# A round-ordered mixer kernel: weight steps ahead of kv's split in every attention round, the gated MLP's PSUM banks a on the other side, and one left operand made in the fourth gated batch

## The chip, the cores and the metric

The kernel runs on one core of one Trainium2 chip. The metric is the device time of one execution in microseconds (us): the median of the runs that are shown. TensorE multiplies matrices, VectorE and ScalarE do elementwise work and read TensorE's results from PSUM, GpSimd does elementwise work in SBUF, and SyncE's queue (SP) issues nearly all transfers. Each engine works through its own instructions in the order in which they were written into its queue, so an instruction that waits holds up all that stands behind it on that engine.

## The reference, cut to what matters

Three layers follow each other, for 8 batches of 576 tokens and 512 channels (8 heads of 64):

```
phi(x) = [exp(p - max|p|), exp(-(p - max|p|))], p = x @ w_phi     # 64 -> 128 features
kv = phi(k)^T v;  z = sum phi(k);  x = (phi(q) kv) / (phi(q) z + 1e-6)
h = relu(x @ w_in); u, v = halves of h; v_n = normalized v
x = (u * (w_spatial @ v_n + b_spatial)) @ w_out
u = x + (U V) mixed over tokens;  out = u + relu(u @ w_ch1) @ w_ch2
```

The weights w_in, w_out, w_ch1, w_ch2 and U, V arrive as 64-bit floats and are turned into pairs of 32-bit halves (a high part in the fp32r format, and the rest as a low part), so that a product becomes three products of halves.

## The kernel before, in words

**Attention** goes through 32 pairs of heads in 35 overlapping rounds, `p` from -1 to 33; "round 9" means p = 9. A round projects k and q of the next pair, builds the features of this pair (`key_features`, `high_part`, `low_part`), accumulates kv in the PSUM tile `pkv` (`key_values`), splits it into a high part on ScalarE (L714) and a low part on VectorE (L715) in `split_key_values`, and multiplies the pairs one and two rounds behind (`outputs`: a group of six products into the PSUM tile `pn`, which is then copied out as `nd`, L738 on VectorE and L740 on ScalarE). Everything in a round is pinned: each engine gets it in the order of the code.

Beside it a list of jobs prepares the weights of the gated MLP, one piece of a weight in each round in four steps that `step(work)` calls at four places of the round. Of a piece of w_in the first step is ScalarE's (`words`, L62), the second VectorE's (`rounded`, three instructions on `bits`: L67, L71, L75), the third ScalarE's (`sized`, L80, which overwrites what L75 reads), the fourth VectorE's last one (L87), a cast on ScalarE (L184) and a subtraction on GpSimd (L187). In rounds 9 to 13 the list `rest` is not empty: it holds the loads of the first batch's input x, whose cast (L974, ScalarE) and subtraction into `xs` (L971, GpSimd) come at the end of a round. In those rounds the second step stood behind kv's split, in the others ahead of it.

At the end of attention (`p == n - 1` and later, n = 32) the first value products of the gated MLP are put between the last rounds (`fill`, into the three PSUM banks of a tile `pa`; (t, half) names token tile and half), and `stats` copies a bank to SBUF (`v`, L1007) and computes its mean and variance.

**The gated MLP** then goes through the 8 batches. For each, `gate` computes four blocks f by two halves c of `u` (8 products `pu`), then the same of the spatial product `pz`, multiplies them (`u`, L1090, VectorE) and splits the result into `g` (L184 on ScalarE, L187). The output product `px` follows, then the small mix over tokens (`pr`, `pt`, `py`). PSUM tiles come from two pools of four banks each: `a` (pu, pz, px, pv, pt) and `b` (py, pr); a pool's tiles take its banks in turn, and a tile waits until its bank's earlier tile has been read.

Between the products, `units` plans the weights of the last layer: at a place (batch, place) a step is emitted, where places 0 to 7 lie behind the eight pu, 8 to 15 behind the eight pz, "x" behind the opened output products, "blocks" behind the second output tile, "m1" and "m2" behind the halves of the mix. A *left operand* m (0 to 7) of w_ch1 is loaded from DRAM (`load`), its sums are made on GpSimd (L569), and two parts are split: ScalarE casts into the one staging buffer `w2s` (L426), VectorE makes the low part (L430), and two stores to `w1x` carry it away. The lists in `left(m, loading, where, early, second)` say where: `early` places the cast and the low part of the 768 columns taken over as they are, `second` those of the 1024 columns of sums. As `w2s` exists once, a cast waits until the stores before it have landed.

**The channel layer** (from about 870 us of the span) reads the left operands back and runs two chained products (ph, pc) to the end.

Of the kernel before, what the change touches and what calls it, by code (L numbers as in the profile page):

```python
# [16 lines left out]
PSUM = bass.MemoryType.PSUM  # L17
# [121 lines left out]
class Mixer:  # L139
# [196 lines left out]
    def units(self):  # L336
# [180 lines left out]
        rest = others + [rows(m + i * self.NM) for m in (5, 6, 7) for i in range(2)]  # L517
# [15 lines left out]
        assert not rest  # L533
        for m, *where in (
# [8 lines left out]
        ):  # L543
            left(m, *where)

# [232 lines left out]
    def attention(self, jobs):  # L778

        nc, n = self.nc, self.B * self.NP
        late, rest, work = 2 * self.NP, [], None
        self.pinned = {}
        self.load(0, "k", 2)
        self.load(0, "q", 1)
        self.load(0, "v", 2)
        none = lambda: None

        def step(f, last=False):

            if f and (last or not getattr(f, "late", False)):
                with self.behind():
                    return f()
            return f

        pa = early = begun = None

        def fill(ks):  # L800
            for t, half in ks:
                self.ahead = True
                self.value_products(0, t, early[t], range(2 * half, 2 * half + 2))
                self.ahead = False

        def stats(t):
            self.ahead = True
            self.statistics(0, t, early[t])
            self.ahead = False

        for p in range(-1, n + 3):
            tag = "pn" if p < n else "kv"
            new, this, old, older = (0 <= i < n for i in (p + 1, p, p - 1, p - 2))
            if p + 2 < n:
                self.load(p + 2, "k", 2)
            if p == n - 1:
                pa = self.pp.tile([P, 12, P], F32, tag="pa", name="pv_0", bufs=1)
                early = [
                    pa[:, 4 * t : 4 * t + 4].rearrange("p u f -> p (u f)") for t in range(3)
                ]  # L820
                fill([(0, 0)])
            elif p == n:
                fill([(2, 0)])
            less = (begun or self.project(p + 1, "k")) if new else none
            begun = None
            side = self.key_values(p, 1) if this else iter(())
            taken = self.outputs(p - 2, 2, side, 6) if older else none
            less()
            taken()
            work = step(work)  # L830
            if this:
                self.transposes(p)
            if p == n:
                fill([(2, 1)])
            taken = self.outputs(p - 2, 3, side, 6, tag) if older else none
            for _ in side:
                pass
            if p + 2 < n:
                self.load(p + 2, "v", 2)
            if new:  # L840
                self.key_features(p + 1, 0)
            if not rest:
                work = step(work)
            taken()
            if older:
                self.undivided(p - 2)
            if this:
                self.split_key_values(p)
            if rest:
                work = step(work)  # L850
            if p == n - 1:
                fill([(0, 1), (1, 0)])
            less = self.project(p + 1, "q") if new else none
            if p + 2 < n:
                self.load(p + 2, "q", 1)
            if this:
                self.high_part(p, 0)
                work = step(work)
                self.low_part(p, 0)
            for i in {n + 1: (), n + 2: (n - 2, n - 1)}.get(p, (p - 3,)):  # L860
                if 0 <= i < n:
                    self.finish(i)
            less()
            if p < 0:
                begun = self.project(1, "k")
            side = self.key_values(p + 1, 0) if new else iter(())
            taken = self.outputs(p - 1, 0, side, 3) if old else none
            for _ in range(3):
                next(side, None)
            taken()  # L870
            if p == n - 1:
                fill([(1, 1)])
            taken = self.outputs(p - 1, 1, side, 6, tag) if old else none
            for _ in side:
                pass
            if this:
                self.high_part(p, 1)
            if new:
                self.key_features(p + 1, 1)
            if this:  # L880
                self.low_part(p, 1)
            if getattr(work, "late", False):
                taken()
                taken = none
            work = step(work, True)
            taken()
            if n - 1 <= p <= n + 1:
                stats(p - n + 1)
            if older:
                self.reciprocals(p - 2)  # L890
            rest = [step(f) for f in rest]
            rest = [f for f in rest if f]
            if jobs and not work:
                work = jobs.pop(0)()
            if 0 <= p - late < self.KD:
                rest.append(self.load_x(0, p - late))
        while work or jobs:
            work = work() if work else jobs.pop(0)()


    def alloc_moe(self, left, right):
        tc, nc, NF, tail = self.tc, self.nc, self.NF, self.tail
        self.ps = {
            x: es.enter_context(
                tc.tile_pool(name=f"ps{x}", bufs=1, space=PSUM, reuse_waits="tile")
            )
            for x, es in (("a", self.ctx), ("b", left))
        }
        mp = self.mp = left.enter_context(tc.tile_pool(name="mp", bufs=1, reuse_waits="tile"))
        self.gs = self.gated(0)  # L910
        mq = self.mq = right.enter_context(tc.tile_pool(name="mq", bufs=1, side="right", reuse_waits="tile"))


        self.vn = [mq.tile([P, self.NST, self.DH], F32R, name=f"vn{i}") for i in range(2)]
# [916 lines left out]
```

## Time and profile before

| what | value |
|---|---|
| median of 3 runs | 1578.63 us (1577.75 to 1579.96) |
| the profiled execution: its time, its span | 1578.13 us, 1576.3 us |
| TensorE busy (matmul) | 1548.2 us, 98% |
| VectorE, ScalarE, GpSimd busy | 1129.6, 874.1, 800.5 us |
| granted TensorE clock, mean | 0.998 |
| mean DMA rate | 213 GB/s |

The span is the stretch from the first to the last profiled instruction; 1.8 us of the execution lie outside it. A busy TensorE is a sum of modelled durations, so the time it was idle, and the name of what ended each idle stretch, say more here than its share. A granted clock of 1.00 is the 2.4 GHz level, 0.50 the 1.2 GHz level.

### The profile page before, as it was taken

What the parts mean: (1) busy time and instruction counts of PE and PEld (TensorE: products, weight loads), DVE (VectorE), ACT (ScalarE), POOL (GpSimd) and SP (SyncE); (2) the same over time, 40 slices, a digit from 0 to 9 for tenths busy, and PEclk for the clock granted to TensorE, in tenths of its full rate; (3) what the DMA queues carried; (4) which work ended last, traced back from release to release, by engine and by line L of the source; (5) the groups of instructions that cost most, each with busy time, mean ns of one, the idle gap of its engine ahead of it and who ended that gap; (6) DMA issues with size and microseconds to landing.
All of it is one profiled execution on the core that took longest, in us unless ns stands there. A gap on an engine that the chain in (4) does not pass through costs nothing.

```text
span 1576.3 us, 30493 instructions
## 1 busy us (share of the span) xinstructions
PE 1548.2 (98%) x11592; PEld 1460.7 (93%) x11592; DVE 1129.6 (72%) x1630; ACT 874.1 (55%) x1647; POOL 800.5 (51%) x602
## 2 busy tenths in 40 slices
PE   8999999999999999999999999999999999999999
PEld 7988888998898898998897999999999999999998
DVE  6787766884687786686777677777666666666666
ACT  6788777884454453454444555555545555554443
POOL 3767776776344554454644644345455533345430
PEclk9999999999999999999999999999999999999999
DMA  5676666763253652443648788878999877777785
GB/s 153 189 201 199 187 200 175 206 176 104 92 168 124 217 181 97 144 154 106 196 149 343 254 275 263 275 253 278 306 321 327 295 246 234 239 240 247 246 298 164
DMA packets 167703, 335.82 MB, mean 213 GB/s; under 512 B 25603, under 2 KB 90755, under 8 KB 164997
## 3 DMA queue, kind: packets, MB, share of 16 engines
q1 hardware_dynamic: 167412, 333.81, 66.1%
q8 instruction: 91, 1.49, 0.4%
q14 instruction: 56, 0.45, 0.1%
q10 hardware_dynamic: 144, 0.07, 0.0%
HBM read 251.20 MB, written 73.02 MB: 206 GB/s over the span
## 4 chain that ended last, share of the span: by engine, by line
PE 58%; DVE 4%; DMA 2%; issue 1%; ACT 1%; POOL 0%; SPq 0%; DVEq 0%; ACTq 0%; POOLq 0%
PE pc L935 22%; PE ph_x L935 13%; PE ph_z L935 6%; PE pv L935 3%; PE ph_y L935 3%; PE pz L935 2%; PE pu L935 2%; PE px L935 2%; DVE w2s L430 1%; PE pt L1160 1%; DMA w1x<-w2s 1%; PE py L1164 1%; PE pv L947 0%; DVE xl L187 0%; PE pz L1086 0%
## 5 line engine op out<-in xcount | busy, mean ns | idle before, releaser
L935 PE MATMUL pc<-hc,w 128*128 128x288 f32 x2568 | 406.0, 295 | 0.0
L935 PEld LDWEIGHTS pc<-hc,w 128*128 128x128 f32 x2568 | 363.1, 188 | 0.0
L682 POOL TENSOR_TENSOR qp<-e,qp 128x576 fp32r<-128x576 f32 x128 | 183.6, 1455 | 116.8 <-ACT e L679 102.4
L187 DVE TENSOR_TENSOR hc<-h,hc 128x576 fp32r<-128x576 f32 x192 | 200.0, 1050 | 35.9 <-ACT hc L184 35.2
L935 PE MATMUL ph_x<-us,cw 128*128 128x288 f32 x1344 | 212.2, 294 | 0.1
L729 PE MATMUL pn<-qp,kv 128*65 128x288 f32 x768 | 205.5, 327 | 6.4 <-ACT nd L740 5.7
L935 PEld LDWEIGHTS ph_x<-us,cw 128*128 128x128 f32 x1344 | 189.4, 188 | 0.7 <-ACT u L1415 0.5
L1348 POOL TENSOR_TENSOR t<-u,t 128x576 f32<-128x576 f32 x32 | 57.7, 1802 | 236.4 <-DVE c L1420 213.7
L1415 ACT COPY u<-ph_x 128x288 f32<-128x288 f32 x128 | 51.2, 400 | 201.4 <-PE ph_x L935 200.9
L1348 POOL TENSOR_TENSOR h<-h,h 128x576 f32<-128x576 f32 x60 | 100.3, 1672 | 110.2 <-DVE r L1623 106.7
L701 PE MATMUL pkv<-v,kp 128*128 128x65 f32 x1024 | 152.4, 251 | 0.0
L701 PEld LDWEIGHTS pkv<-v,kp 128*128 128x128 f32 x1024 | 150.8, 190 | 0.0
L184 ACT CAST hc<-h 128x576 fp32r<-128x576 f32 x192 | 128.6, 672 | 5.4 <-PE pc L935 3.8
L1430 ACT ACTIVATE h<-c 128x288 f32<-128x288 f32 x192 | 85.2, 443 | 68.0 <-DVE c L1420 68.0
L935 PE MATMUL pz<-wt,vn 128*128 128x288 f32 x768 | 115.8, 301 | 4.9 <-DVE u L1090 4.9
L935 PEld LDWEIGHTS pz<-wt,vn 128*128 128x128 f32 x768 | 108.2, 192 | 5.9 <-DVE u L1090 5.9
L729 PEld LDWEIGHTS pn<-qp,kv 128*65 128x65 f32 x768 | 98.1, 138 | 11.4 <-ACT nd L740 8.2
L935 PE MATMUL ph_z<-us,cw 128*128 128x288 f32 x672 | 107.1, 295 | 0.1
L935 PEld LDWEIGHTS pu<-xs,wi 128*128 128x128 f32 x768 | 102.8, 188 | 1.2 <-DVE v L1011 0.5
L935 PE MATMUL pu<-xs,wi 128*128 128x288 f32 x768 | 103.5, 295 | 0.3 <-DVE v L1011 0.3
L1623 DVE TENSOR_TENSOR r<-pc,r 128x576 f32<-128x576 f32 x108 | 81.4, 754 | 28.8 <-PE pc L935 28.6
L1019 POOL TENSOR_TENSOR rstd<-rstd,mhalf 128x1 f32<-128x1 f32 (+1 forms) x40 | 30.7, 769 | 138.7 <-DVE rstd L1018 138.7
(180 smaller groups left out, 3266.3 us busy)
## 6 DMA issues: line engine op xcount, KB each, us to landing
w<-w2d SPq DMA_DIRECT2D x214, 512.0 KB, 4.5
u<-ud SPq DMA_DIRECT2D x16, 1152.0 KB, 8.4
raw_c<-in_w_ch SPq DMA_DIRECT2D x32, 512.0 KB, 4.0
v<-in_v SPq DMA_DIRECT2D x32, 325.0 KB, 4.4
k<-in_kT SPq DMA_DIRECT2D x32, 320.0 KB, 3.5
q<-in_qT SPq DMA_DIRECT2D x32, 320.0 KB, 4.1
x<-nd SPq DMA_DIRECT2D x64, 144.0 KB, 3.4
rec<-rd SPq DMA_DIRECT2D x64, 144.0 KB, 3.3
```

The lines of the kernel that those rows point to most:

```text
L184: self.put(nc.scalar.copy(hi, src))
L187: return self.put((nc.gpsimd if elo == "pool" else nc.vector).tensor_tensor(out=lo, in0=src, in1=hi, op=ALU.subtract))
L430: nc.vector.tensor_tensor(out=d[:, 1, k], in0=x, in1=d[:, 0, k], op=ALU.subtract)
L682: self.pin(nc.gpsimd.tensor_tensor(out=lo[:, c], in0=e[:, c], in1=hi[:, c], op=ALU.subtract))
L701: self.pin(nc.tensor.matmul(pkv[:, i, j, :], kp[:, j * NF + t, :], vb[:, u * D1 : (u + 1) * D1], start=False, stop=(j == 1 and t == NF - 1),))
L729: self.pin(nc.tensor.matmul(pn, kv[k][:, i, g // 2, :], qp[q][:, i, g * HS : (g + 1) * HS], start=(m == 0), stop=(m == len(terms) - 1),))
L935: self.put(self.nc.tensor.matmul(out, x, y, start=(start and i == 0), stop=(stop and i == len(terms) - 1), skip_group_check=chained,))
L1019: put(nc.gpsimd.tensor_tensor(out=rstd[:n], in0=rstd[:n], in1=self.mhalf[:n, :1], op=ALU.pow))
L1348: x = self.put(engine.tensor_tensor(out=out, in0=p, in1=q, op=ALU.subtract))
L1415: self.put(nc.scalar.copy(out, src))
L1430: self.put(nc.scalar.activation(self.h[n, t // 2, x][:, t % 2], src, AF.Relu))
L1623: self.read = self.put(nc.vector.tensor_tensor(out=r, in0=pc, in1=r, op=ALU.add)).ins
```

## The change

Four edits: in rounds 9 to 13 VectorE's weight step moves ahead of kv's split; the products (2, 0) and the first copy to `v` change places in what the last full round writes down; pool `a` is laid from PSUM's other end, and pool `b` takes its place; and the places of the left operands change (m = 1's second part three places later; m = 4 takes new places in batch 3, m = 5 the former ones of m = 4, m = 6 nearly those of m = 5, m = 7 starts where m = 6 did).

```diff
--- before.py
+++ after.py
@@ -533,13 +533,13 @@
         assert not rest
         for m, *where in (
             (0, (1, "blocks"), (1, "m2"), ((1, "m2"), (1, "m2")), ((2, 2), (2, 3))),
-            (1, (2, 1), (2, 4), ((2, 5), (2, 6)), ((2, 8), (2, 9))),
+            (1, (2, 1), (2, 4), ((2, 5), (2, 6)), ((2, 11), (2, 12))),
             (2, (2, 10), (2, 15), ((2, 15), (2, "x")), ((2, "m1"), (2, "m1"))),
             (3, (2, "blocks"), (2, "m2"), ((2, "m2"), (2, "m2")), ((3, 2), (3, 3))),
-            (4, (3, "blocks"), (3, "m2"), ((3, "m2"), (3, "m2")), ((4, 2), (4, 3))),
-            (5, (6, 13), (6, 15), ((6, 15), (6, "x")), ((6, "m2"), (6, "m2"))),
-            (6, (7, 0), (7, 2), ((7, 2), (7, 3)), ((7, 5), (7, 6))),
-            (7, (7, 5), (7, 8), ((7, 8), (7, 9)), ((7, 11), (7, 12))),
+            (4, (3, 14), (3, "x"), ((3, "x"), (3, "x")), ((3, "m1"), (3, "m1"))),
+            (5, (3, "blocks"), (3, "m2"), ((3, "m2"), (3, "m2")), ((4, 2), (4, 3))),
+            (6, (6, 13), (6, 15), ((6, "x"), (6, "x")), ((6, "m2"), (6, "m2"))),
+            (7, (7, 0), (7, 2), ((7, 2), (7, 3)), ((7, 8), (7, 9))),
         ):
             left(m, *where)
 
@@ -819,8 +819,6 @@
                     pa[:, 4 * t : 4 * t + 4].rearrange("p u f -> p (u f)") for t in range(3)
                 ]
                 fill([(0, 0)])
-            elif p == n:
-                fill([(2, 0)])
             less = (begun or self.project(p + 1, "k")) if new else none
             begun = None
             side = self.key_values(p, 1) if this else iter(())
@@ -839,15 +837,12 @@
                 self.load(p + 2, "v", 2)
             if new:
                 self.key_features(p + 1, 0)
-            if not rest:
-                work = step(work)
+            work = step(work)
             taken()
             if older:
                 self.undivided(p - 2)
             if this:
                 self.split_key_values(p)
-            if rest:
-                work = step(work)
             if p == n - 1:
                 fill([(0, 1), (1, 0)])
             less = self.project(p + 1, "q") if new else none
@@ -884,6 +879,8 @@
                 taken = none
             work = step(work, True)
             taken()
+            if p == n - 1:
+                fill([(2, 0)])
             if n - 1 <= p <= n + 1:
                 stats(p - n + 1)
             if older:
@@ -902,9 +899,9 @@
         tc, nc, NF, tail = self.tc, self.nc, self.NF, self.tail
         self.ps = {
             x: es.enter_context(
-                tc.tile_pool(name=f"ps{x}", bufs=1, space=PSUM, reuse_waits="tile")
+                tc.tile_pool(name=f"ps{x}", bufs=1, space=PSUM, side=side, reuse_waits="tile")
             )
-            for x, es in (("a", self.ctx), ("b", left))
+            for x, es, side in (("a", self.ctx, "right"), ("b", left, "left"))
         }
         mp = self.mp = left.enter_context(tc.tile_pool(name="mp", bufs=1, reuse_waits="tile"))
         self.gs = self.gated(0)
```

VectorE's queue in round 9 (`kv_9` is the low part of that pair's kv; `bits_wi` is the weight step; `mk`, `sk`, `mq`, `sq` reduce and shift the projections of k and q). Before:

```order
L637 TENSOR_REDUCE mk_1414<-pk_1391 128x9
L640 TENSOR_TENSOR sk_1415<-pk_1391,mk_1414 128x1152
L715 TENSOR_TENSOR kv_9_1452<-pkv_1344,kv_9_1451 128x260
L67 TENSOR_SCALAR bits_wi_1_1455<-raw_wi_1_1384 128x256
L71 SCALAR_TENSOR_TENSOR bits_wi_1_1455<-raw_wi_1_1384,bits_wi_1_1455 128x256
L75 ISA bits_wi_1_1455<-bits_wi_1_1455,low_wi_1_1419 128x512
L637 TENSOR_REDUCE mq_1481<-pq_1459 128x9
L640 TENSOR_TENSOR sq_1482<-pq_1459,mq_1481 128x1152
```

and now:

```order
L637 TENSOR_REDUCE mk_1414<-pk_1391 128x9
L640 TENSOR_TENSOR sk_1415<-pk_1391,mk_1414 128x1152
L67 TENSOR_SCALAR bits_wi_1_1445<-raw_wi_1_1384 128x256
L71 SCALAR_TENSOR_TENSOR bits_wi_1_1445<-raw_wi_1_1384,bits_wi_1_1445 128x256
L75 ISA bits_wi_1_1445<-bits_wi_1_1445,low_wi_1_1419 128x512
L715 TENSOR_TENSOR kv_9_1456<-pkv_1344,kv_9_1455 128x260
L637 TENSOR_REDUCE mq_1481<-pq_1459 128x9
L640 TENSOR_TENSOR sq_1482<-pq_1459,mq_1481 128x1152
```

The three instructions on `bits` moved from behind kv's low part to ahead of it, straight behind `sk`. Rounds 10 to 13 read the same.

TensorE's queue at the end of attention, with the semaphores that it waits for (rows `pv_4433` are halves of the value products into `pa`: the first two shown open the half (2, 0), the one after `pn_2` the half (2, 1); `pv_3` is the first tile in pool a). Before:

```order
L729 MATMUL pn_1_4520<-qp_30_4378,kv_30_4363 65x288 x2
L935 MATMUL pv_4433<-wi_111,xs_1386 128x512 [waits Activation_49]
...
L729 MATMUL pn_2_4553<-qp_30_4377,kv_30_4363 65x288 [waits DVE_49]
...
L935 MATMUL pv_4433<-wi_111,xs_1386 128x512
...
L729 MATMUL pn_3_4621<-qp_31_4497,kv_31_4480 65x288 x2
L935 MATMUL pv_3_4691<-wi_111,xs_1386 128x512 [waits Activation_49]
```

and now:

```order
L729 MATMUL pn_1_4520<-qp_30_4378,kv_30_4363 65x288 x2
L932 MATMUL pv_4433<-wi_111,xs_1386 128x512
...
L729 MATMUL pn_2_4553<-qp_30_4377,kv_30_4363 65x288 [waits DVE_49]
...
L932 MATMUL pv_4433<-wi_111,xs_1386 128x512 [waits Activation_49]
...
L729 MATMUL pn_3_4621<-qp_31_4497,kv_31_4480 65x288 x2
L932 MATMUL pv_3_4691<-wi_111,xs_1386 128x512
```

The products stand as they did. The wait for ScalarE has moved from the half (2, 0) to the half (2, 1), which stands six `pn` products further on, and the one at `pv_3` is gone.

ScalarE's queue in the gate of batch 7 (`u` and `g` as above; `w2s` is the staging buffer, filled from `w_7` or `z_7` of the left operand; `low_c` and `raw_c` are weight pieces). Before:

```order
L1064 ACTIVATE u_3_9563<-pu_3_1_9585 128x288
L184 CAST g_9606<-u_0_9439 128x288
L426 CAST w2s_9633<-w_7_9558 128x768
L184 CAST g_9606<-u_0_9439 128x288
L116 ACTIVATE low_c_15_9654<-raw_c_15_9579 128x512
L117 ACTIVATE raw_c_15_9579<-raw_c_15_9579 128x512
L184 CAST g_9606<-u_1_9479 128x288 x2
L426 CAST w2s_9702<-z_7_9628 128x1024
L184 CAST g_9606<-u_2_9519 128x288 x2
L184 CAST g_9606<-u_3_9563 128x288 x2
L957 COPY gt_9780<-g_9606 128x4x64 x2
```

and now:

```order
L1061 ACTIVATE u_3_9576<-pu_3_1_9597 128x288
L184 CAST g_9616<-u_0_9459 128x288
L426 CAST w2s_9638<-z_7_9514 128x1024
L184 CAST g_9616<-u_0_9459 128x288
L116 ACTIVATE low_c_15_9659<-raw_c_15_9592 128x512
L117 ACTIVATE raw_c_15_9592<-raw_c_15_9592 128x512
L184 CAST g_9616<-u_1_9499 128x288 x2
L184 CAST g_9616<-u_2_9539 128x288 x2
L184 CAST g_9616<-u_3_9576 128x288 x2
L954 COPY gt_9780<-g_9616 128x4x64 x2
```

One cast into the staging buffer is left where there were two, and it now takes the second part of m = 7; its first part (`w_7`) moved up among the eight `u`, to the place where that of m = 6 was. In the gate of batch 2, likewise, the cast `w2s<-z_1` moved from behind the first `g` cast to behind the fourth `g` cast and the second `xs` cast. In batch 3 a cast `w2s<-w_4` now stands ahead of the first copy of `px` (L1124).

## Rows read from the trace of the kernel before

**Rows 1.** Who waited for whom, TensorE: us in total, times, longest us.
```profile
PE pn L729 <- ACT nd L740: 5.7, 7, 1.2
PE pz L935 <- DVE u L1090: 4.9, 2, 3.0
```

**Rows 2.** Stretch table: length, busy us by engine, clock, DMA share, GB/s.
```profile
900.00:1000.00 100.00, 100.00 (x758) 100.00 (x757) 73.01 (x94) 53.59 (x116) 49.08 (x31) 1.00 0.84 270
```

**Rows 3.** Timeline, TensorE, attention: start, us, engine, line, tiles, count, [idle before <-releaser].
```profile
82.42 0.49 PE L694 MATMUL pkv<-v,kp 128*128 128x130 f32 x2 [0.38 <-DVE kv L715]
118.03 0.34 PE L729 MATMUL pn<-qp,kv 128*65 128x288 f32 x1 [0.88 <-ACT nd L740]
165.13 0.35 PE L729 MATMUL pn<-qp,kv 128*65 128x288 f32 x1 [1.19 <-ACT nd L740]
174.83 0.49 PE L694 MATMUL pkv<-v,kp 128*128 128x130 f32 x2 [0.87 <-DVE kv L715]
```

**Rows 4.** Timeline, round 9: VectorE and ScalarE.
```profile
114.50 0.43 DVE L715 TENSOR_TENSOR kv<-pkv,kv 128x260 fp32r<-128x260 f32 x1 [2.13 <-ACT kv L714]
115.62 0.42 DVE L75 CUSTOM_DVE_ANT_0 bits_wi<-bits_wi,low_wi 128x512 uint16<-128x512 uint16 x1
116.14 0.44 ACT L80 ACTIVATE low_wi<-raw_wi 128x256 f32<-128x256 f32 x1 [0.64 <-DVE bits_wi L75]
```

**Rows 5.** Timeline, round 14: GpSimd and VectorE.
```profile
172.56 1.59 POOL L971 TENSOR_TENSOR xs<-x,xs 128x576 fp32r<-128x576 f32 x1
173.03 1.41 DVE L75 CUSTOM_DVE_ANT_0 bits_wi<-bits_wi,low_wi 128x512 uint16<-128x512 uint16 x1
174.36 0.41 DVE L715 TENSOR_TENSOR kv<-pkv,kv 128x260 fp32r<-128x260 f32 x1
```

**Rows 6.** Timeline, the border from attention to the gated MLP.
```profile
366.00 1.67 PE L935 MATMUL pv<-wi,xs 128*128 128x512 f32 x6 [0.93 <-ACT v L1007]
374.89 3.04 PE L935 MATMUL pv<-wi,xs 128*128 128x512 f32 x12 [1.07 <-ACT v L1007]
376.88 0.21 DVE L761 RECIPROCAL den<-den 128x9 f32<-128x9 f32 x1 [3.11 <-DMA den<-nd]
```

**Rows 7.** Timeline, gate of batch 2: all engines and SP's queue.
```profile
516.16 0.85 SPq L550 DMA_DIRECT2D w1x<-w2s  x2
520.55 1.76 PE L935 MATMUL pz<-wt,vn 128*128 128x288 f32 x12
522.42 1.76 PE L935 MATMUL pz<-wt,vn 128*128 128x288 f32 x12
523.68 1.05 ACT L426 CAST w2s<-z 128x1024 fp32r<-128x1024 f32 x1 [5.16 <-DMA w1x<-w2s]
525.91 0.45 DVE L1090 TENSOR_TENSOR u<-pz,u 128x288 f32<-128x288 f32 x1
526.41 2.41 PE L935 MATMUL pz<-wt,vn 128*128 128x288 f32 x12 [1.97 <-DVE u L1090]
531.91 11.09 PE L935 MATMUL px<-wo,g 128*128 128x512 f32 x48
```

**Rows 8.** Stretch table, TensorE alone: busy us, clock, DMA share, GB/s.
```profile
528.00:530.00 2.00, 2.00 (x9) 0.50 0.88 244
```

**Rows 9.** Timeline, gate of batch 7.
```profile
820.05 1.05 ACT L426 CAST w2s<-z 128x1024 fp32r<-128x1024 f32 x1 [1.66 <-POOL z L569]
828.30 1.76 PE L935 MATMUL pz<-wt,vn 128*128 128x288 f32 x12
831.03 0.83 ACT L426 CAST w2s<-w 128x768 fp32r<-128x768 f32 x1 [6.63 <-DMA w1x<-w2s]
833.27 2.11 PE L935 MATMUL pz<-wt,vn 128*128 128x288 f32 x12 [2.95 <-DVE u L1090]
838.62 11.06 PE L935 MATMUL px<-wo,g 128*128 128x512 f32 x48
```

**Rows 10.** Timeline, ScalarE in the output product of batch 3.
```profile
599.69 1.95 ACT L1124 COPY x<-px 128x512 f32<-128x512 f32 x3 [2.31 <-PE px L935]
```

## The prediction

> **What bounds the kernel now.** I read the table of stretches first. TensorE is busy nearly everywhere, and in the channel layer wholly: 100.00 of 100 us between 900 and 1000 us, at full clock [rows 2]. What is saved ahead of 900 us should therefore end the run earlier by as much, and nothing in this change touches the work after it. So I looked only for stretches before 900 us in which TensorE is idle, by the list of waits [rows 1] and then, place by place, the timeline. Two entries matter. Its products `pn` wait for ScalarE's copy `nd`, 5.7 us in 7 waits; and its products `pz` wait for VectorE's `u`, 4.9 us in only two waits. Both lie at places that the change touches, and so do two waits at the border of attention [rows 6].
>
> **Part 1: the weight step in rounds 9 to 13.** In round 9 VectorE is idle for 2.13 us ahead of kv's low part, since that needs ScalarE's cast; only then come the three instructions on `bits`; ScalarE's L80, which overwrites what the last of them reads, is held for 0.64 us [rows 4]; the copy `nd` behind it on ScalarE comes late, and TensorE waits 0.88 us [rows 3]. Two rounds cost about 0.88 each, three about 1.19 [rows 3]. In round 14 the step already stands ahead of kv, and there it has a cost of another kind: GpSimd's `xs` subtraction runs beside it, L75 takes 1.41 us instead of 0.42, kv's low part starts behind it at 174.36, and TensorE waits 0.87 us for it at `pkv` [rows 3 to 5]. Sum of these six waits: 2 x 0.88 + 3 x 1.19 + 0.87 = 6.2 us.
>
> After: the `bits` fit into the 2.13 us gap. In rounds 9 and 10 no `xs` runs; the nearest rows are rounds 1 to 8, which have the step in the early place: four short waits in all of them, the longest 0.38 [rows 3]. I leave 0.2 for each. In rounds 11 to 14 an `xs` subtraction follows in each, as round 14 shows. The upper bound is 0.87 in each of the four, the lower 0.2 as in the early rounds. I take 0.5: a TensorE wait at `pkv` delays the next round's projection of k, and so the `bits`, while GpSimd's chain goes on, so the next round should meet `xs` nearer to its end. Left: 0.4 + 2.0 = 2.4 us; **gain 3.8**, with bounds 6.2 - 3.9 = 2.3 and 6.2 - 1.2 = 5.0.
>
> A rule speaks against this part. The row shows L75 at 1.41 us, ending at 174.44, where `xs` ended at 172.56 + 1.59 = 174.15 [rows 5]. The Trainium skill (SBUF — State Buffer, "Who interferes with whom") says that a VectorE instruction with two SBUF inputs and a GpSimd instruction that reads SBUF exclude each other, and that the later one stands still until the earlier has finished. The trace agrees in this row. By it every round with `xs` would be like round 14 if its `bits` start as early; that case is rival A below, worked out there from rows.
>
> **Part 2: the border to the gated MLP.** The half (2, 0) waited 0.93 us, and `pv_3` 1.07 us, each for a copy `v` on ScalarE [rows 6]. The first wait moves to (2, 1); the copy that was awaited at 366.00 is then one product group of 1.67 us and six `pn` in the past, so it costs nothing. The second was a wait for the banks of `pa`, which lie elsewhere now; what follows, `pv_4`, needs only a cast that ScalarE makes beside it. What could take the time back is the chain through VectorE that normalizes `v`: its reciprocal at 376.88 waited 3.11 us for a transfer [rows 6]. That transfer `den` stood behind `rec` in SP's queue and now stands ahead of it, so this chain should come earlier too. **Gain 2.0**; lower bound 1.1, if one of the two is given back at a later `v`; upper 2.3.
>
> **Part 3: batch 2.** The stores of `w1x` were issued at 516.16; ScalarE reached the next cast into `w2s` at once but could start it only at 523.68, after 5.16 us of idling; the `g` and, on VectorE, the `u` behind it came late; the PSUM bank of that `u` came free only after 525.91, and TensorE waited 1.97 us [rows 7]. The wait is not the whole price. Granted clock between 528 and 530 us was 0.50 [rows 8], the lower level, after TensorE had stood idle. From `pz` to `pz` an undisturbed step is 522.42 - 520.55 = 1.87 us; the last three `pz` before `px` took 531.91 - 522.42 = 9.49 us where 3 x 1.87 = 5.61 would do. So this place cost 3.9 us, half of it clock. The cast now stands behind four `g` casts and two `xs` casts, which keep ScalarE at work until about when the stores land. If they don't land before 523.68 again, ScalarE still idles for some time, but the `u` of the first four `pz` no longer stand behind it. VectorE must still do its 1.2 us low part among the later `u`. **Gain 3.4**, with 3.9 as the upper bound and 2.0 as the lower (the wait itself back, half as long, at the first `px`).
>
> **Part 4: batch 7.** The same at a cast for m = 7: 6.63 us of ScalarE idling for the stores of m = 6's second part, 2.95 us on TensorE, and 838.62 - 828.30 - 5.61 = 4.7 us lost in all [rows 9]. Now only one cast stands among the `g`, and the stores that it needs are those issued among the `pu`: in the trace the cast after those, at 820.05, was already free of them and waited for GpSimd [rows 9]. The cast now comes some 4 us later than that, so it should not wait at all. **Gain 4.5**; upper bound 4.7 plus 0.4 that TensorE waits at `pr` behind it, lower 2.0 if the longer second part (1.05 us on ScalarE, as much on VectorE) holds up the first `px` or the reading in of the channel layer's operands.
>
> **Part 5: what batch 3 takes on.** Four loads, four sums, two casts (0.83 and 1.05 us, as in [rows 7, 9]), two low parts and four stores. The cover: ScalarE idles 2.31 us ahead of the first copies of `px` at 599.69 [rows 10], where the first cast lands; the second comes in the mix, where batch 2 has had one without a wait of TensorE. Without the cover the cost is at most the two casts, 1.9 us, at `px`. I take **0.2 lost**. Batches 6 and 7 are relieved by as much.
>
> **Sum.** 3.8 + 2.0 + 3.4 + 4.5 - 0.2 = 13.5 us. The profiled execution took 1578.13 us (its span is 1576.3), 0.5 below the median 1578.63. So 1564.6 on its scale, 1565 as a median. The five lower bounds sum to 2.3 + 1.1 + 2.0 + 2.0 - 1.9 = 5.5 (1573), the upper ones to 5.0 + 2.3 + 3.9 + 5.1 = 16.3 (1562).
>
> **Rivals.**
> A. Rounds 11 to 14 all cost the 0.87 us of round 14 [rows 3], and the border gives only 1.1: 2.3 + 1.1 + 3.4 + 4.5 - 0.2 = 11.1, so 1567.5. For it: L75 ended just behind `xs` [rows 5]. Against: the lag of one round helps the next.
> B. One of the two long waits stays, because VectorE, not the store, is what is late: its `bits` of the weight pieces, the low part and the `u` follow without a gap. Then 13.5 less about 4 gives 9.5, so 1569. For it: after the late start at 525.91 VectorE needed until `px` to catch up. Against: both times ScalarE's idling, 5.16 and 6.63 us, came first [rows 7, 9].
> C. Slower: landing of the stores. If stores to `w1x` take 7.5 us and more, as from 516.16 to 523.68 [rows 7], also in the new places, then the casts in batch 2, batch 3 (two), batch 6 and batch 7 each wait, and each such wait costs TensorE about 4.3 us with its clock (the mean of 3.9 and 4.7). Five give 21.5 where 8.6 were before: 12.9 lost against 5.8 from parts 1 and 2, so 1586. It decides from four such places on (17.2 - 8.6 = 8.6 over 5.8). Against: the new distances are longer, and ScalarE has idle time at three of them.
> D. Nothing arrives at the end, as the channel layer keeps to its loads (DMA share 0.84 [rows 2]): 1576 to 1580. Against: TensorE's 100.00.
>
> **Chances.** Forecast 0.58, A 0.17, B 0.14, C 0.05, D 0.06. This kernel's measurement can tell about 0.2% (3.2 us) from no change. Faster holds the forecast, A and B: 0.89; same D: 0.06; slower C: 0.05. The range 1561 to 1572 leaves out C, D and the worst ends of the forecast and B.
>
> **What would show it.** Right: no wait of `pn` over 0.3 us in rounds 9 and 10, waits at `pkv` between 0.2 and 0.9 in rounds 11 to 14; no `pv` wait at the border; eight `pz` at 1.87 us steps in batches 2 and 7 and a clock of 1.00 throughout. Wrong: a `pz` or `px` wait of 2 us or more in batches 2, 3 or 7 (B, C), or a channel layer that starts 13 us earlier and ends less early (D).

## The result and the profile after

The changed kernel takes 1563.30 us (1562.45 to 1565.45, 4 runs), the kernel before 1578.19 us (4 runs, 3 of them those shown ahead). The ratio is 0.9903, interval 0.9889 to 0.9917: 15 us faster. Forecast were 1565.0 us, range 1561 to 1572. The profiled execution took 1562.45 us with a span of 1560.7 us. Lines of the changed kernel are lower by 3 behind L887 (L1090 is L1087 now, L971 is L968).

First TensorE's waits in the list of who waited for whom (us in total, times, longest us), which answers to [rows 1]:

```profile
PE pk L628 <- DMA wst<-in_w_phi: 4.1, 1, 4.1
PE pkv L694 <- DVE kv L715: 3.4, 8, 0.9
PE px L932 <- POOL g L187: 1.2, 1, 1.2
...
PE px L944 <- ACT x L1121: 0.8, 1, 0.8
PE pr L1137 <- DVE xl L187: 0.6, 3, 0.2
PE pq L628 <- PE pn L729: 0.6, 1, 0.6
PE pn L729 <- ACT nd L740: 0.6, 3, 0.2
```

The 5.7 us of `pn` for `nd` have become 0.6, the 4.9 us of `pz` for `u` are gone, and so are both `pv` waits. New are `px` for GpSimd's `g` (0.2 us before) and, in rounds 11 to 13, `pkv` for kv's low part; in round 14 that wait has shrunk from 0.87 to 0.39 us. The `pkv` waits of rounds 11 to 14 are in the timeline (start, us, engine, line, tiles, count, [idle before <- what ended it]); the two rows ahead of them belong to round 11:

```profile
134.32 1.58 POOL L968 TENSOR_TENSOR xs<-x,xs 128x576 fp32r<-128x576 f32 x1
134.78 1.41 DVE L75 CUSTOM_DVE_ANT_0 bits_wi<-bits_wi,low_wi 128x512 uint16<-128x512 uint16 x1
136.58 0.49 PE L694 MATMUL pkv<-v,kp 128*128 128x130 f32 x2 [0.88 <-DVE kv L715]
147.89 0.49 PE L694 MATMUL pkv<-v,kp 128*128 128x130 f32 x2 [0.39 <-DVE kv L715]
159.19 0.49 PE L694 MATMUL pkv<-v,kp 128*128 128x130 f32 x2 [0.40 <-DVE kv L715]
170.49 0.49 PE L694 MATMUL pkv<-v,kp 128*128 128x130 f32 x2 [0.39 <-DVE kv L715]
```

L75 takes 1.41 us beside `xs`, as in [rows 5], now in rounds 11 to 14. Batch 2 in the timeline, which answers to [rows 7]:

```profile
509.47 1.98 SPq L964 DMA_DIRECT2D x<-xd  x2
515.64 0.67 ACT L971 CAST xs<-x 128x576 fp32r<-128x576 f32 x1 [2.72 <-DMA x<-xd]
518.73 1.05 ACT L426 CAST w2s<-z 128x1024 fp32r<-128x1024 f32 x1
520.22 2.42 POOL L968 TENSOR_TENSOR xs<-x,xs 128x576 fp32r<-128x576 f32 x1
520.46 2.02 PE L932 MATMUL px<-wo,g 128*128 128x512 f32 x8
522.60 2.19 POOL L187 TENSOR_TENSOR g<-u,g 128x288 fp32r<-128x288 f32 x2
523.63 9.36 PE L932 MATMUL px<-wo,g 128*128 128x512 f32 x40 [1.15 <-POOL g L187]
```

The cast at 518.73 waits for no store. But ScalarE now idles 2.72 us for the next batch's x; GpSimd's `xs` are therefore late, the two `g` of block 2 stand behind one of them, and `px` waits 1.15 us.

Each part can be measured between marks. The ordinary table below is worked out from starts of instructions in the timelines of all profiled kernels, those of the experiments included: the mean stretch where the part has its old code, and where it has its new code, with the number of profiles.

```
stretch                                        old code      new code     won
kv's low part, round 8 to round 15             81.26 (7)     78.08 (4)    3.2
kv's low part of round 31 to px of batch 0     48.15 (5)     44.76 (7)    3.4
batch 2, first pz to first px                  18.32 (6)     15.08 (4)    3.2
batch 2, first px to next pu                   33.22 (6)     34.92 (4)   -1.7
px of batch 3 to px of batch 6                179.81 (7)    179.83 (4)    0.0
batch 7, first pz to first px                  19.85 (6)     14.92 (7)    4.9
batch 7, first px to first pc                  45.41 (6)     43.78 (7)    1.6
```

Together 14.6 us. The mix of batch 6, whose casts also moved, takes the same from its first px to the next pu: 34.4 us with the old rows (7 profiles) and with the new ones (4). The channel layer passes the gain on: from the first `pc` to the end 692.0 us before (1576.3 - 884.27) and 692.1 after (1560.7 - 868.58).

### The profile page after: what moved, and what is told of

Its sections match the earlier page's. It is cut to its first block, busy times and chain, and to the rows that moved or that the text cites. A ratio compares the mean times of both kernels' runs of the same rounds, so it can differ in the third digit from the quotient of the medians.

```text
span 1560.7 us, 30489 instructions
## 1 busy us (share of the span) xinstructions
PE 1543.3 (99%) x11592; PEld 1457.9 (93%) x11592; DVE 1136.9 (73%) x1630; ACT 875.5 (56%) x1647; POOL 801.9 (51%) x602
## 4 chain that ended last, share of the span: by engine, by line
PE 85%; DMA 5%; DVE 4%; ACT 3%; issue 1%; SPq 1%; POOL 0%; DVEq 0%; ACTq 0%; POOLq 0%
PE pc L932 22%; PE ph_x L932 13%; PE ph_z L932 6%; PE pu L932 6%; PE pv L932 5%; PE pz L932 5%; PE pn L729 5%; PE px L932 4%; PE pkv L701 4%; PE ph_y L932 3%; PE pk L628 2%; PE pt L660 1%; PE pq L628 1%; PE pt L1157 1%; DMA den<-nd 1%
```

## The experiments

In the first five, a part of the change stands alone in the kernel before.

**Weight step alone.**

```diff
-            if not rest:
-                work = step(work)
+            work = step(work)
...
-            if rest:
-                work = step(work)
```

> The kernel before with the weight step alone in its new place in rounds 9 to 13 (nothing else changed). My theory: the waits of pn for the copy nd go, and in rounds 11 to 14 a wait of pkv for kv's low part of 0.9 us once and 0.4 us three times stands in their place, so 6.2 - 2.2 = about 4.0 us less (1574.5 us). Rival A (each of the four rounds costs 0.87 us): 2.3 us less. A rival that the order in these rounds does not reach the end, since later rounds have slack: within 1 us of before.

Measured: 1574.89 us, ratio 0.9982 [0.9973, 0.9992], 2.8 us less. Its profile has rounds 8 to 15 at 78.10 us, as the full change has (78.23). The interval (1.3 to 4.3 us) holds my 4.0 as well as rival A's 2.3, so the ratio does not part them. The profile does: `pkv` waits 0.87 us once and then 0.39, 0.41 and 0.39 us, as in my theory, and not four times 0.87 us.

**m = 1's second part alone.**

```diff
-            (1, (2, 1), (2, 4), ((2, 5), (2, 6)), ((2, 8), (2, 9))),
+            (1, (2, 1), (2, 4), ((2, 5), (2, 6)), ((2, 11), (2, 12))),
```

> The kernel before with one edit: the second part of left operand m = 1 in batch 2 at (2, 11) and (2, 12) in place of (2, 8) and (2, 9). My theory: the gate of batch 2 gets 3.9 us shorter with the clock at 1.00 through it, and 1.2 to 1.7 us come back as a wait of the first px for GpSimd's low part g, so 2.2 to 2.7 us less (1576 us). Rival B (VectorE is late by itself): a pz wait of 2 us stays and nothing is won. A rival that the px wait has nothing to do with this edit: the full 3.9 us are won.

Measured: 1576.47 us, 0.9994 [0.9981, 1.0007], which does not tell it from no change. The profile does tell: the gate of batch 2 takes 14.93 us, `px` then waits 1.40 us for `g`, and from there to the next `pu` 34.92 us pass. So 3.9 us are won against the profile of before (3.4 against the mean of the table) and 1.9 given back. The rival of a full gain falls, rival B too.

**Two stores that don't read the staging buffer.**

```diff
+                    d = h["d"][:, i] if own else self.wi[i][:, :, :HALF]
-                    self.stores.append((dst(i, slice(x0, x0 + h["n"])), h["d"][:, i, : h["n"]].bitcast(F32)))
+                    self.stores.append((dst(i, slice(x0, x0 + h["n"])), d[:, : h["n"]].bitcast(F32)))
...
-            part(lambda: [w[0][:, :3]], dst, 0, early)
-            part(lambda: [z[0]], dst, 3, second)
+            part(lambda: [w[0][:, :3]], dst, 0, early, m != 1)
+            part(lambda: [z[0]], dst, 3, second, m != 6)
```

> The kernel before with its old table; only the stores of two parts (m = 1's first part in batch 2, m = 6's second part in batch 7) take their data from the persistent weights wi instead of the staging tile w2s, so the next cast into w2s need not wait for their landing. The same bytes, casts and VectorE work; what is left out is that these two parts of w1x hold the right numbers. My theory (the landing of the stores holds the cast on ScalarE): ScalarE's idle times of 5.16 and 6.63 us ahead of the two casts go, both pz waits (1.97 and 2.95 us) and the low clock go, 7 to 8.6 us less (1570.5 us). Rival B (VectorE, with its bits, low part and u in a row, is late by itself): the pz waits stay, within 1 us of before.

Measured: 1576.43 us, 0.9991 [0.998, 1.0001]: far less than the 7 to 8.6 us expected. ScalarE in its timeline (batch 2, then batch 7):

```profile
518.62 1.05 ACT L426 CAST w2s<-z 128x1024 fp32r<-128x1024 f32 x1
822.86 0.83 ACT L426 CAST w2s<-w 128x768 fp32r<-128x768 f32 x1
834.60 1.05 ACT L426 CAST w2s<-z 128x1024 fp32r<-128x1024 f32 x1 [5.21 <-DMA w1x<-w2s]
```

Both disputed casts start without a wait, no `pz` waits anywhere, and the gates take 15.17 and 16.23 us where the profiles with the old code take 18.3 and 19.9 in the mean. So the landing of the stores was the cause, and rival B falls. But in batch 7 the next cast, for m = 7's second part, now idles 5.21 us for the stores ahead of it: `px` waits 1.1 us for `u`, 0.4 and 0.8 us for `g`, and the tail takes 48.30 us instead of 45.4. The stall went one cast further. In the changed kernel the parts of m = 6 and m = 7 stand further apart, and the one cast left among the `pz` of batch 7 (813.91) idles for nothing.

**The table's rows m = 4 to 7 alone.** The edit is the last four rows of the table's diff, shown ahead.

> The kernel before with only the table rows of left operands m = 4 to 7 changed (m = 4 into batch 3's 14, x and m1; m = 5, 6 and 7 each one row earlier, m = 7's second part at (7, 8) and (7, 9)). My theory: the gate of batch 7 falls from 19.6 to 14.9 us, its tail up to the channel layer by 1.9 us, batch 3 pays nothing: 5 to 6.6 us less (1571.5 us). Rival C: stores that have not landed hold the casts in batch 3 and batch 6, 2 to 4 us each come back, so 0 to 3 us less. A rival that the gain of the tail came from elsewhere (the earlier parts): 4.7 us less only.

Measured: 1570.56 us, 0.9957 [0.9945, 0.9969], 6.8 us less. Gate of batch 7 14.93 us, tail 43.77, batch 3 unchanged: the gain of the tail belongs to this part.

**The border, both edits, then each alone.**

```diff
-            elif p == n:
-                fill([(2, 0)])
...
+            if p == n - 1:
+                fill([(2, 0)])
             if n - 1 <= p <= n + 1:
                 stats(p - n + 1)
...
-                tc.tile_pool(name=f"ps{x}", bufs=1, space=PSUM, reuse_waits="tile")
+                tc.tile_pool(name=f"ps{x}", bufs=1, space=PSUM, side=side, reuse_waits="tile")
-            for x, es in (("a", self.ctx), ("b", left))
+            for x, es, side in (("a", self.ctx, "right"), ("b", left, "left"))
```

Both: 

> The kernel before with only the two border edits: the half (2, 0) filled one round earlier in the text, and the banks a on PSUM's other side. My theory: both pv waits (0.93 and 1.07 us) go, the first pu comes 2.0 to 2.4 us earlier, and as the chain that normalizes v is earlier too, the first px of batch 0 comes 3.0 to 3.3 us earlier: about 3 us less (1574.5 us). Rival A's half: one wait comes back at a later v, 1.1 us less. A rival that ScalarE's v copies are the bound there whatever the banks: 0.

Fill alone: 

> The kernel before with the fill of the half (2, 0) alone moved (PSUM sides as before). My theory: the pv wait of 0.93 us goes or is spent elsewhere on the way to pu, the one of 1.07 us for the banks stays: pu 0.9 us earlier, 0.9 to 1.2 us less in all (1576.3 us). Rival: with the banks unchanged the next pv waits longer by what the first saved: 0.

Sides alone: 

> The kernel before with only the banks a of the gated MLP on PSUM's other side (fill as before). My theory: the pv wait of 1.07 us goes, the one of 0.93 us stays: pu 1.1 to 1.4 us earlier, and with it the chain that normalizes v, 1.1 to 2 us less in all (1575.8 us). Rival: pv_4 then waits for ScalarE's cast in its place: 0.

Measured: both 0.9983 [0.9973, 0.9993]; fill alone 0.9983 [0.997, 0.9996]; sides alone 1.0001 [0.9989, 1.0012]. The profiles are sharper: from kv of round 31 to the first `px` 48.2 us as before, 44.76 with both, 46.08 with the fill, 49.66 with the sides. So the sides alone lose 1.5 us in their one profile (the interval of their ratio allows up to 1.9). Their timeline, and a row of the stretch table for TensorE alone in it (length, busy us, clock, DMA share, GB/s):

```profile
376.77 0.21 DVE L761 RECIPROCAL den<-den 128x9 f32<-128x9 f32 x1 [3.49 <-DMA den<-nd]
376.90 1.51 DVE L186 CAST vn<-v 128x512 fp32r<-128x512 f32 x1
384.84 9.72 PE L935 MATMUL pu<-xs,wi 128*128 128x288 f32 x60 [2.11 <-DVE v L1011]
```

```profile
386.00:388.00 2.00, 2.00 (x10) 0.50 0.02 8
```

and, in the timeline, the reciprocal with both edits, which waits for nothing:

```profile
372.27 0.21 DVE L761 RECIPROCAL den<-den 128x9 f32<-128x9 f32 x1
```

With the sides alone the wait of 1.07 us goes, but the reciprocal stays where it was [rows 6], the chain that normalizes `v` stands behind it on VectorE, and `pu` waits 2.11 us for it; the granted clock is then 0.70 between 384 and 386 us, 0.50 up to 388 and 0.95 up to 390. With the fill moved, SP issues the transfer `den` ahead of `rec` (369.76 and 371.35 us with both edits; with the sides alone `rec` at 372.73, `den` at 374.27), the reciprocal is 4.5 us earlier, and the 1.07 us are really won. The fill alone is worth 2.1 us in its profile (0.9 to 1.2 expected), and both together 3.4 (3.0 to 3.3 expected); the ratios do not part these two. For the sides my 1.1 to 2 us fall; the ratio is the rival's 0, but the reason is this chain and not `pv_4`.

**xs eight rounds later.** In the changed kernel:

```diff
-        late, rest, work = 2 * self.NP, [], None
+        late, rest, work = 4 * self.NP, [], None
```

> The changed kernel with the loads and splits of batch 0's x eight rounds later, so that GpSimd's xs subtractions stand in rounds 19 to 22, which have no bits steps. My theory (L75 and xs hold each other off, and kv's low part stands behind L75): L75 in rounds 11 to 14 falls from 1.41 to about 0.43 us, the pkv waits there (0.88, 0.39, 0.40, 0.39) go, 2.0 us less than the changed kernel (ratio to before 0.989). Rival 1: L75 is slow for another reason, or the waits come from the chain of kv itself: 0 us against the changed kernel (0.9903). Rival 2: xs beside VectorE's wt casts makes new waits of the same size in rounds 19 to 22: also 0, but with L75 at 0.43.

Measured: 1563.93 us, 0.991 [0.9892, 0.9928]: no difference from the changed kernel. Round 12 (147.4) and then rounds 17 and 18, between their low parts of kv:

```profile
147.43 0.43 DVE L75 CUSTOM_DVE_ANT_0 bits_wi<-bits_wi,low_wi 128x512 uint16<-128x512 uint16 x1
147.77 0.42 DVE L715 TENSOR_TENSOR kv<-pkv,kv 128x260 fp32r<-128x260 f32 x1
208.86 0.80 DVE L186 CAST wt<-w_wt 128x576 fp32r<-128x576 f32 x1 [2.64 <-DMA w_wt<-in_w_spT]
212.86 1.16 PE L628 MATMUL pq<-wst,q 64*128 64x128 f32 x16 [1.52 <-issue]
```

L75 is at 0.43 us, no `pkv` wait is left in rounds 11 to 14, and rounds 8 to 15 take 75.94 us, 2.1 less than after. So the mechanism is shown. From there to round 23 91.6 us pass instead of 88.4: `pq` waits three times, 1.52, 1.09 and 1.09 us. Ahead of the first two VectorE idles 2.64 and 2.10 us at the cast of `w_wt`, ahead of the third 2.66 us at the reciprocal for `den`: transfers that land late. Rival 2 stands in its size, not in its reason: the first of these waits comes 12 us ahead of the first `xs`, which now starts at 225.18.

**The changed kernel again.** 

> The changed kernel unaltered, a second profile of it beside more runs. My theory: the terms of the sum repeat to a few tenths of a us (gate of batch 2 at 14.9 us and of batch 7 at 14.9 us from the first pz to the first px, weight step rounds with 0.4 us at pkv), while three waits for landings differ from profile to profile by 1 to 2 us: pq in rounds 17 to 20 (w_wt), the last px of batch 6 (x), the first px of batch 2 (g). In all 1563 to 1565 us. A rival: the single profiles are too unlike to be read by parts, then the gates differ by more than 1 us.

Measured: 1562.77 us, 0.991 [0.9897, 0.9923]. Gates 15.29 and 14.92 us, `pkv` 0.86, 0.39, 0.42 and 0.38 us, `px` in batch 2 1.42 us: single profiles can be read by parts to some 0.4 us. In this profile `pq` waits 1.15 us at 235.05, and the granted clock then falls to 0.50 for some 3 us, so that the clock is not 1.00 throughout in every execution of the changed kernel. Waits for landings are less steady: `px` for the copy x in batch 6 was 0.2 us in the profile of before, 1.0 to 2.0 in those of the six experiments that keep its old table, 0.8 and 0.5 in the two of the changed kernel, and 1.5 and 1.0 in the two other profiles with its rows for m = 6.

**Two more places of the table.** In the changed kernel:

```diff
-            (1, (2, 1), (2, 4), ((2, 5), (2, 6)), ((2, 11), (2, 12))),
+            (1, (2, 1), (2, 4), ((2, 5), (2, 7)), ((2, 11), (2, 12))),
...
-            (6, (6, 13), (6, 15), ((6, "x"), (6, "x")), ((6, "m2"), (6, "m2"))),
+            (6, (6, 13), (6, 15), ((6, "blocks"), (6, "blocks")), ((6, "m2"), (6, "m2"))),
```

> The changed kernel with two more edits of its table: m = 1's low part and stores in batch 2 one step later, at (2, 7), so that SP issues the loads of the next batch's x ahead of those stores, and m = 6's first part at batch 6's blocks instead of x, so that its cast stands behind two copies x on ScalarE. My theory: the first px of batch 2 no longer waits 1.2 us for g and the px of batch 6 no longer waits 0.8 us for x; from px to pu in these two mixes 34.7 and 34.0 us fall towards the 32.2 us of the undisturbed ones: 2 to 4 us less than the changed kernel (1560 us, ratio to before 0.988). Rival: m = 1's stores now land later than the second cast at (2, 11) comes up, ScalarE idles there, and the pz wait of batch 2 with its low clock is back: 0 to 2 us more than the changed kernel.

Measured: 1558.89 us, 0.9885 [0.9872, 0.9899], faster than the changed kernel on the same chip (0.991) by some 4 us. Batch 2:

```profile
508.49 0.92 SPq L964 DMA_DIRECT2D x<-xd  x2
509.52 2.56 SPq L550 DMA_DIRECT2D w1x<-w2s  x2
513.82 0.67 ACT L971 CAST xs<-x 128x576 fp32r<-128x576 f32 x1 [0.63 <-DMA x<-xd]
516.92 1.05 ACT L426 CAST w2s<-z 128x1024 fp32r<-128x1024 f32 x1
```

The loads of x stand ahead of the stores in SP's queue; the cast `xs` waits 0.63 us instead of 2.72, and no `px` wait is left in the whole profile. The stretch from `px` to `pu` falls to 32.96 us in batch 2 (33.65 and 33.69 in the two later kernels with this table), and in batch 6 from 34.4 to 32.5. The rival, stores that land too late for the cast, did not come.

**xs in the middle of the round.** On top of the last kernel: `load_x` marks its second step (`rest.mid = True`), and the round takes it there.

```diff
                 self.low_part(p, 0)
+            rest = [f for f in rest if not (getattr(f, "mid", False) and [step(f)])]
```

> The kernel of the last run (changed kernel with the two table edits, 1558.9 us, ratio 0.9885), and GpSimd's four xs subtractions of rounds 11 to 14 issued in the middle of their rounds, between qp's low part and the product x by rec, in place of the rounds' end; VectorE's and ScalarE's order is the same. My theory (L75 and xs hold each other off where they meet): L75 in rounds 11 to 14 falls from 1.41 to between 0.43 and 0.8 us (GpSimd's wi subtraction of 0.79 us now runs last there), the pkv waits of 0.86, 0.41, 0.37, 0.38 us go, 1.5 to 2 us less (1557.2 us, 0.9875). Rival 1: moving xs only moves the hold, to VectorE's mq or sk instructions of those rounds, which the next pk and pq need: 0. Rival 2: GpSimd's finished x and second qp part, 1.6 us later, hold TensorE's pn: 1 us or more lost.

Measured: 0.9887 [0.9865, 0.9908], no gain; rounds 8 to 15 take 78.74 us, 0.7 more. The first rows are round 11, the last three round 12:

```profile
133.67 2.83 POOL L682 TENSOR_TENSOR qp<-e,qp 128x576 fp32r<-128x576 f32 x2
135.26 1.52 DVE L71 SCALAR_TENSOR_TENSOR bits_wi<-raw_wi,bits_wi 128x256 int32<-128x256 int32 x1
136.92 0.73 DVE L75 CUSTOM_DVE_ANT_0 bits_wi<-bits_wi,low_wi 128x512 uint16<-128x512 uint16 x1
144.00 0.21 DVE L761 RECIPROCAL den<-den 128x9 f32<-128x9 f32 x1 [1.81 <-DMA den<-nd]
148.90 0.43 DVE L75 CUSTOM_DVE_ANT_0 bits_wi<-bits_wi,low_wi 128x512 uint16<-128x512 uint16 x1
149.71 0.49 PE L694 MATMUL pkv<-v,kp 128*128 128x130 f32 x2 [0.75 <-DVE kv L715]
```

The hold moved one instruction ahead, from L75 (1.41 to 0.73) to L71 (0.84 to 1.52), which meets GpSimd's second `qp` part now: rival 1 in kind, at another instruction than it named. In round 12 nothing is held, yet `pkv` waits 0.75 us, since the reciprocal ahead of `sk` waited 1.81 us for its transfer. My expectation failed.

**xs four rounds later.** The same line as in the eight rounds' move, with `3 * self.NP`, in the kernel with the two table edits.

> The changed kernel with the two table edits of the run of 1558.9 us (ratio 0.9885), and batch 0's x loaded and split four rounds later (not eight): GpSimd's xs subtractions stand ahead of kv in rounds 15 to 18, of which only round 15 has bits on VectorE, and SP issues the loads of x ahead of those of w_wt. My theory (the hold of L75 by xs made 2.1 us of pkv waits in rounds 11 to 14, and the eight rounds' move lost its gain because the w_wt transfers then shared the queue with x's loads): L75 at 0.43 us in rounds 11 to 14, one pkv wait of 0.4 to 0.9 us in round 15, no pq waits over 0.6 us in rounds 17 to 20: 1.2 to 1.6 us less (1557.4 us, 0.9876). Rival: any xs split in rounds with w_wt work makes pq wait there as after eight rounds' move (three waits of 1.1 to 1.5 us): 0 to 2 us more.

Measured: 1559.03 us, 0.9879 [0.9862, 0.9895], no difference from 0.9885. L75 is at 0.42 us up to round 14, and rounds 8 to 15 take 76.69 us instead of 78.08, with 0.87 us at round 15 as expected. Then:

```profile
181.63 0.49 PE L694 MATMUL pkv<-v,kp 128*128 128x130 f32 x2 [0.87 <-DVE kv L715]
203.87 0.49 PE L694 MATMUL pkv<-v,kp 128*128 128x130 f32 x2 [0.38 <-DVE kv L715]
237.01 1.16 PE L628 MATMUL pq<-wst,q 64*128 64x128 f32 x16 [1.21 <-issue]
```

Up to round 23 all is given back in this profile (166.17 us from round 8, against 165.57). Whether this is `xs` or the scatter of the `w_wt` landings stays open: `pq` waits of 0.5 to 1.4 us stand in several profiles that have `xs` at its first place.

## Why the prediction was right, and where its terms were off

The sum was 13.5 us, the measured ratios give 14 to 15. It came out close because terms that were too low and too high balance, and that is in part luck: parts 2 and 4 gave more than their upper bounds (2.3 and 5.1), part 3 less than its lower one (2.0).

- **Part 1, 3.8 forecast, 3.2 measured.** The waits came in the size that was argued: none over 0.2 us in rounds 9 and 10, 0.88 and then three of 0.4 us at `pkv`. The left wait is 2.1 us, 2.4 forecast. What was off is the left side: six idle times of 6.2 us in sum were not 6.2 us of delay. Against the 75.94 us that these rounds take with nothing held, those of before lose 5.3. Rival A's repeated 0.87 us did not come. The reason given for that does not hold as it was put, though: the next round should have met `xs` nearer to its end. In all four rounds L75 starts 0.46 us behind `xs` and takes 1.41 us. The lag is taken up earlier, at L67, the first instruction on `bits`. Rounds 11 and 12 after the change:

```profile
130.84 2.78 POOL L682 TENSOR_TENSOR qp<-e,qp 128x576 fp32r<-128x576 f32 x2
132.68 1.09 DVE L67 TENSOR_SCALAR bits_wi<-raw_wi 128x256 int32<-128x256 int32 x1
142.12 2.79 POOL L682 TENSOR_TENSOR qp<-e,qp 128x576 fp32r<-128x576 f32 x2
144.47 0.59 DVE L67 TENSOR_SCALAR bits_wi<-raw_wi 128x256 int32<-128x256 int32 x1
145.62 1.59 POOL L968 TENSOR_TENSOR xs<-x,xs 128x576 fp32r<-128x576 f32 x1
146.08 1.41 DVE L75 CUSTOM_DVE_ANT_0 bits_wi<-bits_wi,low_wi 128x512 uint16<-128x512 uint16 x1
```

  L67 ends 0.15 us behind GpSimd's `qp` in both. As VectorE comes to it later against GpSimd from round 12 on, it takes 0.5 us less, and by about that much the wait at `pkv` is shorter (0.39 for 0.88). The row of round 11 bears on the rule of the Trainium skill that the prediction weighed (SBUF — State Buffer, "Who interferes with whom"): L75 ends at 136.19, GpSimd's `xs` at 135.90. With `xs` elsewhere L75 takes 0.43 us, and with GpSimd's `qp` in its place L71 ends at 136.78, `qp` at 136.50: the traces agree.
- **Part 2, 2.0 forecast, 3.4 measured.** The step that failed is the split into one wait for each edit. The two depend on each other: the transfer order `den` ahead of `rec`, which the prediction named as a help, is the condition for the gain of the PSUM sides. The upper bound of 2.3 was too low since what is lost behind the border was left out of it: in the profile of before, 0.6 us in the `pu` of batch 0 and 0.4 in its `pz`, against the one with both edits.
- **Part 3, 3.4 forecast, 1.5 measured.** The gate gained its 3.2 to 3.9 us. The case of the lower bound (a wait at the first `px`) is what happened, but at a price of 1.7 us, which puts the gain under that bound of 2.0. I had looked for what the cast would wait for, and not for what waits behind the stores in SP's queue: the loads of x, then `xs`, then `g`. The working's "half of it clock" does not hold either. In four of the six profiles that keep the old batch 2 the clock stayed at 1.00 behind this wait. Weight step alone, with a row of the stretch table for TensorE alone:

```profile
522.09 1.86 PE L932 MATMUL pz<-wt,vn 128*128 128x288 f32 x12 [1.74 <-DVE u L1087]
524.87 1.85 PE L932 MATMUL pz<-wt,vn 128*128 128x288 f32 x12 [0.65 <-DVE u L1087]
527.37 6.83 PE L932 MATMUL px<-wo,g 128*128 128x512 f32 x29 [0.38 <-DVE u L1087]
```

```profile
524.00:526.00 2.00, 1.35 (x10) 1.00 0.93 265
```

  Two more waits for VectorE's `u` follow here. From the end of the first wait to the first `px` 5.28 or 5.29 us pass in these four, and 5.50 and 5.34 in the two at the lower clock, where the slower products fill the same time. So the clock cost 0.1 to 0.2 us, and the rest of the price beyond the first wait comes from VectorE's late `u` in the next two steps.
- **Part 4, 4.5 forecast, 6.6 measured.** The gate's 4.9 us are the 4.7 that were read; all six profiles with the old code fall to the lower clock there, so what the clock costs in this gate stays open. The tail was under-sized at 0.4, and stood in the upper bound alone: before, the six `pr` take from 851.37 to 854.19 us, after from 837.59 to 838.95, 1.5 us less, while only 0.45 us of that was shown as idle.
- **Part 5, 0.2 lost forecast, 0.0 measured.** The cover held.
- **Rivals.** B is excluded by the two stores that read another tile. C came in one of its five places, at another price: ahead of the cast at batch 6's "x" ScalarE idles 4.21 us for stores, those of another weight to `w2d` (3.75 us ahead of that place's cast before), and TensorE's wait for the copy x behind it is 0.8 us, not 4.3. The casts that moved in batches 2, 3 and 7 waited for no store. D is excluded by the 692 us of the channel layer.

## What to carry to other kernels

Price a stall by the stretch from a mark ahead of it to a mark behind it, against the same stretch undisturbed: the idle times beside it were too much in one place (6.2 for 5.3 us) and too little in two (1.97 for 3.9, 0.45 for 1.5). Before a loss is put down to the clock, look for a profile with the same wait at the full clock. When a wait for a staging buffer is taken away, look at once at the next cast on the same buffer and at what stands behind its stores in the queue; here one such move sent the wait to the next cast, and another to transfers behind the stores. Two edits whose waits lie on one chain are not to be added: one of them lost 1.5 us alone and won 1.3 us beside the other, by one profile each.

## What the runs showed of the hardware

- VectorE's cast `vn` took 1.51 us at 376.90 (PSUM sides alone), where GpSimd multiplied x from 376.69 on for 1.43 us, and 0.42 us where nothing ran beside it (377.59 with both border edits). L67 took 1.09 and 0.59 us and ended 0.15 us behind GpSimd's `qp` both times. Both read one tile: not only instructions with two inputs are held.
- TensorE's granted clock stayed at 1.00 through waits of 1.15 and 1.42 us at the first `px` of batch 2, and fell to 0.50 after one of 2.11 us at `pu` and one of 1.97 us [rows 7, 8]. The length of the one wait does not decide it: it stayed at 1.00 through 1.97 us at `px` of batch 6 (783.33, two stores from another tile), and fell after 1.15 us at `pq` (235.05, second profile of the changed kernel).
- The price of the lower clock depends on what the products wait for next. From `pu` to the first `pz` of batch 0 the sides alone take 16.59 us and both border edits 12.73: 3.9 us lost, 1.75 of them beyond the wait of 2.11. In the gate of batch 2, where VectorE was late in any case, it was 0.1 to 0.2 us. A wait with the clock at 1.00 can cost more than its length too: that of 1.15 us cost 1.0 to 1.8 (34.72 against the 32.96 to 33.69 us without it).
- Taking away the only `px` waits of batch 2 and batch 6 was worth 3.4 us by the two stretches (1.5 and 1.9), as much as the border or the weight step, though both together were 2.0 us in the list of waits.
